# All scores in 64x64 tiles, key tails of four heads in one round, loads and engine order rearranged: cosine attention with a highway FFN behind it

## The chip, the cores and the metric

One core of one Trainium2 chip. The core has five engines that run their own instruction streams in order: PE (TensorE, matrix products; PEld is its weight load), DVE (VectorE), ACT (ScalarE), POOL (GpSimd) and SP (SyncE, here only a queue that starts transfers). A wait of an instruction holds up all that stands behind it on its engine. The metric is the device time of one execution in microseconds, the median over runs.

## The reference

Eight batches of twelve heads, 448 tokens, head dimension 64. Then a highway layer over the 3584 token rows of 768 numbers.

```python
q_n = q / (norm(q, axis=-1) + 1e-06);  k_n = k / (norm(k, axis=-1) + 1e-06)
scores = matmul(q_n, k_n^T) / tau                       # tau = 0.1
attn = softmax(scores);  a = matmul(attn, v)            # (8, 12, 448, 64)
x = a.transpose(0, 2, 1, 3).reshape(3584, 768)
H = maximum(x @ w_h, 0);  T = sigmoid(x @ w_t + b_t)    # 768 x 768 weights
out = T * H + (1 - T) * x
```

## The kernel before, in words

**Layout.** A head's 448 tokens are laid out as token = 7 l + j, with l = 0..63 on partitions and j = 0..6 (`NJ`) along the row. Two heads that differ in their last bit (s = 0, 1) share the 128 partitions. The twelve heads of a batch are three quads (g = 0..2); a quad holds the heads (t, s) with t, s = 0, 1. A pair p is the two heads t = 0, 1 at one s: six pairs a batch. Normalised and turned, a quad's queries and keys (`qT`, `kT`) have the two heads t on the two halves of the 128 partitions (64 numbers each) and tokens along the row.

**Stages of a batch.** Load q (started by SP), k and v (started by POOL, cast to half precision on the way; batch 0's k comes in full precision into `E` buffers by `ld_kf`). Squares on ACT (`norm`, `sq`), sums on DVE, the inverse root by Ln and Exp on ACT in batch 0 (`lnexp`) and by Newton steps on DVE else. `scale` multiplies q and k by it, mostly on POOL (`qn`, `kn`), for each quad in two halves t. `turn` transposes them: on PE with a copy by DVE, or by a transposing transfer in late batches (`QDMA`, `KDMA`). `scores` makes the products of keys and queries into PSUM banks (`B`, eight of them), ACT takes their exponentials into `E`; `attend` multiplies these with the values (`vp`, with a column of ones that yields the sum) on PE, and DVE divides. Batch 0 has its own versions (`attend0`) that cut the queries into four parts i. `ffn` then works on four row tiles a batch: it turns x, multiplies with `wt` and `wh` on PE, ACT takes a tanh, DVE and POOL combine, SP stores.

**Scores.** The 448 keys of a head are three chunks of 128 (c = 0..2) and a tail of 64. For each chunk of a pair, L496 issues two products of 64 rows by 128 columns, one for each head, on the two row halves of the array ("T" in the code). The tails of the pair go in one product over the whole array (L507): the keys' tail is held as a 128x128 block with zeros beside the two heads' parts, which is why `kn` has eight blocks of j, two half empty, that `zkn` fills with zeros, and why the scaling of k is two instructions (four and three blocks of j). Its exponentials are one tile `Et` a pair. In `attend`, each group c of query rows takes one product with `Et` over 130 columns (both heads at once, L521) and six with `E` over 65 columns (L526); the last 64 query rows go on column halves of the array ("C", L534). FFN products are whole-array (L682), its tail tiles on column halves (L679).

**Order.** All operations are recorded in a `Plan` with numbers, and `ORDER`, a table of these numbers made beforehand by a search, sets the order on every engine; `SLOTS` sets which buffer each tile takes. At emission some operations are also made to wait for one on another engine (`behind`): loads of q behind the latest ACT operation, a POOL operation behind the latest DVE operation, by two general rules.

**Counters of transfers.** In the built program each transfer that POOL starts raises one of eight counters, DMASW0 to DMASW7, in turn, and SP's and ACT's transfers use DMAHW0 to DMAHW7 in the same way. The ninth transfer takes the first counter again, and its instruction waits until the first transfer has landed.

**Start.** `WARM` = 18 products on zeros (`wz`) and `NF` = 39 further ones (L305) stand between the first real products of PE.

Of the kernel before, what the change touches and what calls it, by code (L numbers as in the profile page):

```python
# [20 lines left out]
66 1 67 342 68 0 69 3 72 71 7 70 5 42 61 339 23 19 75 74 64 21 44 52 20 51 22 55 79 9 83 43 2 6 14 13 81 82 73 80 8 85  # L21
86 16 84 15 63 39 341 87 76 88 12 95 96 60 108 25 33 56 31 11 38 24 107 46 89 40 114 113 17 37 109 32 4 90 53 30 111
10 97 18 112 98 93 115 118 110 353 54 116 174 91 137 124 117 94 357 92 29 142 173 175 28 122 105 123 99 340 177 59 119
180 354 121 100 125 120 133 127 128 349 141 126 48 138 26 34 350 154 58 178 347 129 140 153 176 131 578 139 144 143
358 78 134 132 130 106 150 149 45 179 348 155 101 102 343 152 151 156 47 77 186 355 57 359 135 189 181 190 182 192 191
351 360 136 361 50 362 183 146 62 104 103 363 364 145 41 147 36 365 148 184 185 187 27 352 383 198 188 158 162 356 377
378 579 161 165 166 157 35 167 164 159 193 194 163 202 49 382 201 345 168 381 379 169 197 195 196 203 204 209 170 160
206 200 199 212 380 210 171 222 172 346 221 205 384 207 266 234 226 208 267 344 211 224 225 233 223 227 366 367 213
809 214 235 286 271 272 385 368 287 369 370 584 215 371 372 581 592 216 236 228 268 291 217 386 269 238 218 404 585
219 387 245 270 237 273 588 593 248 220 246 229 403 393 240 239 292 430 230 288 247 416 388 242 231 398 293 65 389 432  # L30
241 392 391 394 583 397 289 589 232 243 279 280 413 274 417 431 290 244 427 306 275 281 429 395 428 307 249 415 410
414 316 317 412 250 396 252 390 586 318 594 401 424 253 587 276 580 582 590 402 450 254 376 277 425 311 255 595 312
278 256 808 260 426 259 411 319 451 294 262 591 375 433 261 1263 373 596 434 251 320 374 407 313 597 295 408 263 441
598 264 599 813 409 257 435 600 436 442 308 309 443 437 812 824 816 299 282 601 602 321 265 310 811 438 447 449 258
607 461 448 611 608 444 825 613 634 300 399 301 418 420 463 446 445 462 439 440 467 609 400 421 458 468 464 419 817
631 460 466 405 614 633 465 296 406 297 459 610 612 621 298 818 326 475 617 481 632 476 483 477 455 422 484 423 454
624 327 615 623 616 478 622 469 618 470 819 485 482 501 453 604 479 480 452 502 498 1036 456 302 500 495 619 472 471
487 499 496 492 486 663 488 603 820 620 606 497 605 494 457 473 489 283 637 640 474 490 491 493 814 815 641 505 625
504 503 642 822 638 639 506 643 507 328 508 528 645 329 646 821 509 626 333 334 644 657 647 304 284 303 664 674 330
628 823 335 651 627 648 650 697 680 649 658 566 547 654 826 659 676 681 675 652 660 532 314 827 810 828 829 1038 662  # L40
331 305 830 834 529 315 1037 1039 831 322 332 530 533 832 336 635 531 1035 655 636 843 698 661 513 656 534 1051 514
677 653 1270 671 323 510 511 540 665 337 541 667 678 515 679 629 512 672 673 837 1052 838 666 542 839 842 840 1043 691
685 859 630 855 1044 668 846 847 850 714 518 669 519 520 516 692 715 856 693 683 682 670 848 535 708 688 694 684 537
1271 538 695 1262 689 710 690 686 521 522 539 728 696 687 709 730 705 711 324 841 1045 712 523 567 707 702 713 568 729
833 536 543 1046 569 706 844 1047 701 731 700 338 551 699 732 703 835 851 725 1041 845 722 552 723 724 1048 553 718
559 560 716 717 544 887 726 870 1042 727 1049 889 704 736 719 735 734 890 852 857 733 720 561 721 325 849 285 858 737
556 557 836 860 738 864 872 871 891 888 777 867 861 558 1050 884 570 869 853 885 1274 572 573 886 854 545 865 866 881
898 571 883 1053 739 1054 517 873 758 874 1266 1055 1056 882 862 1057 1058 868 1490 1060 1059 548 863 549 924 900 899
550 892 894 877 876 1067 796 901 904 574 1275 895 878 740 893 1268 1065 1076 546 1087 1264 875 575 879 896 741 903 902
925 524 743 576 907 762 905 1272 526 1278 525 742 897 880 744 770 906 554 918 1279 915 555 908 771 763 916 759 527  # L50
1276 745 1040 1273 1064 760 1073 917 764 1070 1074 748 761 919 920 772 749 1066 1075 932 1082 1505 921 938 751 752 934
933 767 909 940 1083 750 910 941 911 1267 1269 1084 768 958 922 923 939 765 753 1277 935 959 562 769 1062 952 912 1280
766 936 929 797 1068 1063 1078 1489 798 913 914 953 937 746 955 949 577 1069 942 928 951 799 1061 781 782 1281 956 957
773 1265 954 950 563 1071 778 779 1072 926 774 927 1501 780 946 963 783 1111 1108 1282 943 945 1100 944 962 1493 564
# [809 lines left out]
```

## Time and profile before

| what | us |
|---|---|
| median of 3 runs | 254.03 (253.97 to 255.05) |
| span of the profiled execution, first to last instruction | 252.9 |
| the median over that span | 1.1 more |
| PE, DVE, ACT, POOL busy | 237.5, 208.0, 211.5, 184.0 |
| mean granted clock of PE | 0.990 |

The profile lists for each engine how long it was busy, the instructions in order of time, and who waited for whom. A busy PE includes products whose result is still under way, so short gaps do not show in its share. The profiled execution has no time of its own beside its span; the 1.1 us lie around it.

### The profile page before, as it was taken

How to read it: one execution, taken by the hardware profiler on the slowest of the kernel's cores; microseconds unless marked ns; L12 is line 12 of the kernel's file. 1: busy time of each engine (PE TensorE's matmuls, PEld its weight loads, DVE VectorE, ACT ScalarE, POOL GpSimd, SP SyncE). 2: the span in 40 equal slices, each digit the busy share in tenths (PEclk: the TensorE clock that was granted, in tenths of full speed). 3: DMA queues.
4: the chain of work that ended last, by engine and by line, in shares of the span. 5: the costliest groups of instructions: out<-in, count | busy, mean ns of one | idle time of the engine just before them, and what ended most of it. 6: DMA issues, size and time to landing. Idle time of an engine off the chain costs nothing.

```text
span 252.9 us, 7457 instructions
## 1 busy us (share of the span) xinstructions
PE 237.5 (94%) x2895; PEld 147.1 (58%) x2895; DVE 208.0 (82%) x462; ACT 211.5 (84%) x421; POOL 184.0 (73%) x261
## 2 busy tenths in 40 slices
PE   5959999999999999989999999999999999999990
PEld 2425776557756665645765566656656655675650
DVE  4977989999999999989899869689767665556983
ACT  3589999999999999989999999999997669981120
POOL 8369599959798979796989775878476983522540
PEclk9997999999999999999999999999999999999998
DMA  6999999999589999999999998999779588745755
GB/s 219 286 270 237 288 259 202 200 271 179 72 104 146 314 264 248 151 223 163 266 157 170 156 114 138 249 207 193 128 129 231 93 135 192 162 127 123 187 147 156
DMA packets 75892, 47.78 MB, mean 189 GB/s; under 512 B 51536, under 2 KB 72656, under 8 KB 75856
## 3 DMA queue, kind: packets, MB, share of 16 engines
q1 hardware_dynamic: 55568, 33.86, 59.2%
q0 software_dynamic: 19856, 12.68, 37.1%
q10 hardware_dynamic: 432, 0.75, 0.8%
q8 instruction: 22, 0.36, 0.6%
q14 instruction: 14, 0.11, 0.1%
HBM read 38.34 MB, written 11.01 MB: 195 GB/s over the span
## 4 chain that ended last, share of the span: by engine, by line
PE 68%; DMA 11%; ACT 8%; DVE 7%; issue 2%; POOL 2%; SPq 0%; DVEq 0%; POOLq 0%; ACTq 0%
PE B L682 26%; PE B L496 10%; PE B L526 8%; DMA xT<-x 7%; PE B L679 5%; PE B L521 3%; DMA E<-in_k_dram 3%; PE B L447 3%; ACT E L502 3%; PE B L534 3%; PE B L507 2%; PE B L573 2%; ACT sq L380 2%; PE B L305 2%; DVE hm L720 1%
## 5 line engine op out<-in xcount | busy, mean ns | idle before, releaser
L502 ACT ACTIVATE E<-B 128x448 f16<-128x448 f32 x252 | 122.8, 612 | 9.6 <-PE B L496 8.6
L682 PEld LDWEIGHTS <-xT 128*128 128x128 f16 x576 | 52.1, 98 | 39.6 <-issue 6.9
L752 POOL TENSOR_TENSOR os<-x,hm 128x384 f32<-128x384 f16 x53 | 47.6, 912 | 29.8 <-DVE hm L747 21.3
L682 PE MATMUL B<-wh,xT 128*128 128x384 f16 x288 | 56.7, 326 | 0.6 <-DMA xT<-x 0.6
L682 PE MATMUL B<-wt,xT 128*128 128x384 f16 x288 | 55.0, 326 | 1.8 <-DMA xT<-x 1.4
L432 POOL TENSOR_TENSOR kn<-kr,y 128x192 f16<-128x192 f16 (+1 forms) x84 | 45.8, 562 | 10.6 <-DVE y L409 6.1
L391 DVE TENSOR_REDUCE n<-sq 128x14 f32<-128x896 f32 (+1 forms) x50 | 51.2, 1039 | 2.8 <-ACT sq L380 2.6
L432 POOL TENSOR_TENSOR qn<-qr,y 128x448 f16<-128x448 f32 x47 | 43.9, 946 | 9.1 <-ACT y L420 4.4
L526 PE MATMUL B<-vp,E 128*128 128x65 f16 x756 | 38.7, 193 | 0.0
L724 ACT ACTIVATE tt<-z 128x768 f16<-128x768 f32 (+1 forms) x32 | 26.3, 821 | 14.6 <-DVE z L711 14.5
L720 DVE SCALAR_TENSOR_TENSOR hm<-B,x 128x384 f16<-128x384 f32 x53 | 28.8, 549 | 8.4 <-PE B L682 3.9
L526 PEld LDWEIGHTS <-E 128*128 128x128 f16 x756 | 33.7, 98 | 3.2
L496 PE MATMUL B<-qT,kT 64*128 64x448 f16 x252 | 34.8, 354 | 0.4 <-DVE hm L720 0.4
L711 DVE TENSOR_TENSOR z<-B,bias 128x384 f32<-128x384 f32 x48 | 25.8, 551 | 9.3 <-PE B L682 6.3
L521 PE MATMUL B<-vp,Et 128*128 128x130 f16 x126 | 28.1, 223 | 0.0
L380 ACT ACTIVATE sq<-qr 128x896 f32<-128x896 f32 (+1 forms) x24 | 24.1, 1022 | 3.5 <-DMA qr<-in_q_dram 3.5
L509 ACT ACTIVATE Et<-B 128x448 f16<-128x448 f32 x42 | 26.1, 631 | 0.4 <-PE B L507 0.4
L542 DVE SCALAR_TENSOR_TENSOR x<-B,rd 128x448 f16<-128x448 f32 x42 | 25.6, 618 | 0.9
L337 POOL DMA_DIRECT2D vr<-in_v_dram x32 | 21.9, 690 | 2.5 <-DVE z L711 2.5
L586 ACT ACTIVATE E<-B 128x512 f16<-128x512 f32 (+1 forms) x42 | 20.6, 607 | 0.9 <-POOL qn L432 0.5
L380 ACT ACTIVATE sq<-kr 128x896 f32<-128x896 f16 x17 | 17.0, 1041 | 1.1 <-DMA kr<-in_k_dram 1.1
L305 PE MATMUL B<-wz 128*128 128x512 f16 x39 | 14.7, 433 | 2.6 <-DVE wz L281 2.6
(81 smaller groups left out, 313.7 us busy)
## 6 DMA issues: line engine op xcount, KB each, us to landing
out_dram<-os SPq DMA_DIRECT2D x47, 192.0 KB, 3.3
qr<-in_q_dram SPq DMA_DIRECT2D x6, 1344.0 KB, 8.3
kr<-in_k_dram POOLq DMA_DIRECT2D x7, 672.0 KB, 11.6
vr<-in_v_dram POOLq DMA_DIRECT2D x16, 192.0 KB, 6.9
qr<-in_q_dram SPq DMA_DIRECT2D x6, 448.0 KB, 10.0
vr<-in_v_dram POOLq DMA_DIRECT2D x16, 144.0 KB, 7.7
out_dram<-os SPq DMA_DIRECT2D x15, 96.0 KB, 3.8
wt<-in_moe_w_t_dram POOLq DMA_DIRECT2D x1, 1152.0 KB, 24.4
```

The costliest lines, as they stand in the source:

```text
L380: nc.scalar.activation(dst, src, AF.Square, scale=sc)
L391: nc.vector.reduce_sum(R("n2", b)[:, c : c + 7 * n], a, axis=AX.X)
L432: ENG[eng].tensor_mul(N[:, :, t, :] if nm == "q" else N[:, lo > 0 : (lo > 0) + 2 * (hi - lo) - 1 : 2, t, :], source(nm, b, g)[:, t, 64 * l ...
L496: nc.tensor.matmul(R("B", ("S", n, c, t))[:, 0:S], lhsT=R("kT", i)[ln, s, 128 * c : 128 * c + 128], rhs=queries(ln), start=True, stop=True)
L502: nc.scalar.activation(R("E", n)[:, at : at + 7, :].rearrange("l j x -> l (j x)"), R("B", ("S", n, c, t))[:, 0:S], AF.Exp)
L509: op("ACT", f"expt {n}", lambda: nc.scalar.activation(R("Et", n).rearrange("l j x -> l (j x)"), R("B", ("St", n))[:, 0:S], AF.Exp), r=[("B ...
L521: nc.tensor.matmul(U[:, 2 * c : 2 * c + 2, :], lhsT=Et[:, 2 * c : 2 * c + 2, :].rearrange("l j x -> l (j x)"), rhs=vp[:, 6:8, 0:65], start ...
L526: nc.tensor.matmul(U[:, 2 * c + t, :], lhsT=E[:, at : at + 2, :].rearrange("l j x -> l (j x)"), rhs=vp[:, 3 * t + m, 0:65], start=False, s ...
L682: nc.tensor.matmul(P[:, 0:MH], lhsT=xT[:, cc, :], rhs=w_[:, cc, MH * mh : MH * mh + MH], start=(cc == 0), stop=(cc == CC - 1))
L720: op("DVE", f"hm {g} {mh}", lambda at=at, sl=sl, mh=mh: nc.vector.scalar_tensor_tensor(out=R("hm", g)[:, sl], in0=R("B", at)[:, 0:MH], sca ...
L724: op("ACT", f"th{nb} {g}", lambda: nc.scalar.activation(R("tt", g)[:, 0:W], R("z", g)[:, 0:W], AF.Tanh, scale=0.5), r=[("z", g), ("t0",)], ...
L752: op(eng, f"out {g} {mh}", lambda sl=sl, mh=mh: ENG[eng].tensor_add(R("os", g)[:, sl], xpart(mh), R("hm", g)[:, sl]), r=[("gg", g), xk], w ...
```

## The change

- Scores: one helper `score` issues four products of 64x64 for each chunk, one on each quarter of the array: head t on the row half t, key half h on the column half h. The 448-column products of a chunk are now four with 64 stationary columns in place of two with 128.
- Tails: the four heads of a quad have their tails done in one such round of four (`tails`, once a quad), into two banks; `Et` is one tile for each t, with the heads s on the partition halves. 42 whole-array products become 21 rounds of four. `vp` holds zeros in the other head's half.
- `attend`: each group c is eight products over 65 columns in place of one over 130 and six over 65.
- k stays in token order: seven blocks of j, no zeros, one scaling instruction for each half t, seven transposes in place of eight, copies of 896 columns in place of 1024, one transposing transfer a quad in place of two.
- Batch 0 scales half t = 0 of every quad on DVE (before: of quad 0 only).
- No further products on zeros (`NF` = 0); the 18 of `WARM` stand together at the start.
- Loads: ACT starts all three loads of batch 0's k, behind its table load (before: one ahead of it, two on SP). q comes in three loads a batch in all batches. v is loaded by s, not by t. POOL starts both weight loads, batch 2's k and two parts of batch 1's v ahead of its first own work, the identity `ident` for the transposes included.
- `ORDER` and `SLOTS` are new, and the two rules for `behind` give way to a table, `BEHIND`.

```diff
-66 1 67 342 68 0 69 3 72 71 7 70 5 42 61 339 23 19 75 74 64 21 44 52 20 51 22 55 79 9 83 43 2 6 14 13 81 82 73 80 8 85
+0 24 285 4 2 14 26 20 9 31 28 7 25 11 8 3 32 21 27 17 16 33 29 12 6 5 30 19 22 13 15 34 18 10 37 39 35 40 515 38 43 41
...
+BEHIND = dict(
...
+63:65 70:39 74:65 82:81 247:757 267:470 282:49 283:51 284:57 318:218 319:312 320:305 321:305 324:308 328:315 332:315
...
-    WARM, NF, NLATE = 18, 39, 2
+    WARM, NF, NLATE = 18, 0, 2
...
-    SCALE = {("q", 0, 0): ("DVE", "POOL"), ("k", 0, 0): ("DVE", "POOL")}
+    SCALE = {(nm, 0, g): ("DVE", "POOL") for nm in "qk" for g in range(NG)}
...
-        qr=(2, [128, 6, 448], FP32), kr=(3, [128, 6, 448], FP16), kn=(3, [128, 8, 2, D], FP16), vr=(2, [128, NH, 256], FP16),
+        qr=(2, [128, 6, 448], FP32), kr=(3, [128, 6, 448], FP16), kn=(3, [128, NJ, 2, D], FP16), vr=(2, [128, NH, 256], FP16),
...
-        Et=(3, [128, 7, 64], FP16), rd=(2, [128, 7], FP32), x=(3, [128, 7, MH], FP16),
+        Et=(4, [128, 7, 64], FP16), rd=(2, [128, 7], FP32), x=(3, [128, 7, MH], FP16),
...
-        for t, jj, j0, n in ((0, 0, 0, 4), (0, 1, 4, 3), (1, 0, 0, 3), (1, 1, 3, 4)):
+        for s, jj, j0, n in ((0, 0, 0, 4), (0, 1, 4, 3), (1, 0, 0, 3), (1, 1, 3, 4)):
...
-            for lo, hi in ((0, 7),) if nm == "q" else ((0, 4 - t), (4 - t, 7)):
...
-                op(eng, f"{nm}n{hi - lo} {b} {g} {t}", fn, r=[token(nm, b, g), ("y", b, nm, g)], w=[(nm + "n", i, t)])
+            op(eng, f"{nm}n7 {b} {g} {t}", fn, r=[token(nm, b, g), ("y", b, nm, g)], w=[(nm + "n", i, t)])
...
+    def score(out, o, w, K, Q, s, c):
+        for t, h in ((0, 0), (1, 1), (0, 1), (1, 0)):
+            ln = slice(64 * t, 64 * t + 64)
+            S_, j = (s, c + h * (4 - s)) if c < NC else (h, 3 + 3 * h)
+            nc.tensor.matmul(out[t][64 * h : 64 * h + 64, o[t] : o[t] + w], lhsT=K[ln, j, S_, :], rhs=Q[ln, :, S_, :], start=True, stop=True)
...
-                for t in range(2):
-                    ln = slice(64 * t, 64 * t + 64)
-                    nc.tensor.matmul(R("B", ("S", n, c, t))[:, 0:S], lhsT=R("kT", i)[ln, s, 128 * c : 128 * c + 128],
-                                     rhs=queries(ln), start=True, stop=True)
+                score([R("B", ("S", n, c, t)) for t in range(2)], (0, 0), S, R("kT", i), R("qT", i), s, c)
...
-            nc.tensor.matmul(R("B", ("St", n))[:, 0:S], lhsT=R("kT", i)[:, s, 384:512], rhs=queries(slice(0, 128)), start=True, stop=True)
+            score([R("B", ("St", i, t)) for t in range(2)], (0, 0), S, R("kT", i), R("qT", i), 0, NC)
...
-            nc.tensor.matmul(U[:, 2 * c : 2 * c + 2, :], lhsT=Et[:, 2 * c : 2 * c + 2, :].rearrange("l j x -> l (j x)"),
-                             rhs=vp[:, 6:8, 0:65], start=True, stop=False)
...
+                for m in range(NC + 1):
+                    lt = E[:, 7 * (2 * m + t) + 2 * c :][:, 0:2] if m < NC else R("Et", (i, t))[:, 2 * c : 2 * c + 2]
...
-                    ld_kf(g, "SP" if g else "ACT")
+                    ld_kf(g, "ACT")
...
-            ld_qk("q", b)
+            for g in range(NG):
+                ld_qk("q", b, [g])
...
-                elif o.held:
-
-                    behind(made[0], act)
...
+                last[o.seq] = made[-1]
+                if o.seq in BEHIND:
+                    behind(made[0], last[BEHIND[o.seq]])
```

**POOL at the start.** The names are those of the kernel: `kr_63` is the first buffer of k (batch 1's), `kr_64` the second (batch 2's), `vr_69` batch 0's v, `vr_70` batch 1's, `qn_83` and `kn_66` the scaled q and k of quad 0, `y_78` the inverse roots. Before:

```order
L322 DMA kr_63<-in_k_dram 128x6x448
L337 DMA vr_69<-in_v_dram 64x6x256 x2
L337 DMA vr_69<-in_v_dram 64x6x192 x2
L342 DMA wt<-in_moe_w_t_dram 128x6x768
L432 TENSOR_TENSOR qn_83<-qr_61,y_78 128x7x64 [waits DMAHW1_49,DVE_49,Activation_49]
L432 TENSOR_TENSOR kn_66<-E_94,y_78 128x4x64 [waits DMAHW0_49,DVE_49]
L432 TENSOR_TENSOR kn_66<-E_94,y_78 128x3x64
L432 TENSOR_TENSOR qn_84<-qr_61,y_78 128x7x64 [waits DMAHW2_49,DVE_49,Activation_49]
```

And now:

```order
L326 DMA kr_63<-in_k_dram 128x6x448
L341 DMA vr_69<-in_v_dram 64x6x192 x2
L341 DMA vr_69<-in_v_dram 64x6x256 x2
L346 DMA wt<-in_moe_w_t_dram 128x6x768
L346 DMA wh<-in_moe_w_h_dram 128x6x768
L326 DMA kr_64<-in_k_dram 128x6x448
L341 DMA vr_70<-in_v_dram 64x6x256 [waits DMASW0_49]
L341 DMA vr_70<-in_v_dram 64x6x192 [waits DMASW1_49]
masks.py:197 MEMSET ident 128x128
masks.py:199 ISA
masks.py:199 AFFINE_SELECT ident<-ident 128x128 [waits Pool_49]
L434 TENSOR_TENSOR qn_83<-qr_61,y_78 128x7x64 [waits DMAHW0_49,Activation_49]
```

Ten transfers stand ahead of POOL's first work in place of six; the ninth waits for the landing of the first (k of batch 1), the tenth for that of the second (the first part of batch 0's v), and the identity and the first scaling stand behind both.

**ACT at the start.** `sq` are squares, `B` a bank of scores whose exponentials go to `E`. Before:

```order
L380 ACTIVATE sq_73<-E_95 128x896 [waits DMAHW3_49]
L417 ACTIVATE tu_82<-n_76,eps 128x28 [waits DVE_49]
L420 ACTIVATE y_78<-tu_82 128x28 [waits Activation_49]
L380 ACTIVATE sq_74<-E_96 128x896 [waits DMAHW4_49]
L380 ACTIVATE sq_75<-kr_63 128x896 [waits DMASW0_49]
L380 ACTIVATE sq_73<-qr_61 128x896 [waits DMAHW5_49]
L380 ACTIVATE sq_74<-kr_63 128x896 [waits DVE_49]
L586 ACTIVATE E_94<-B_124 128x512 [waits PE_49]
```

And now:

```order
L384 ACTIVATE sq_73<-E_95 128x896 [waits DMAHW3_49]
L384 ACTIVATE sq_74<-qr_61 128x896 [waits DMAHW4_49]
L421 ACTIVATE tu_82<-n_76,eps 128x28 [waits DVE_49]
L424 ACTIVATE y_78<-tu_82 128x28 [waits Activation_49]
L384 ACTIVATE sq_75<-E_96 128x896 [waits DMAHW5_49]
L576 ACTIVATE E_94<-B_127 128x384 [waits PE_49]
L384 ACTIVATE sq_73<-kr_63 128x896 [waits DMASW0_49]
L576 ACTIVATE E_95<-B_123 128x512 [waits PE_49,Pool_49]
```

The first exponential has moved ahead of all squares of batch 1's k, which before filled ACT until PE's first scores were there.

**PE at a tail, in the middle of the program.** Before, a tail stands among whole-array products of the FFN:

```order
L682 LDWEIGHTS xT_108
L682 MATMUL B_124<-wt,xT_108 128x384
L507 LDWEIGHTS kT_90
L507 MATMUL B_122<-qT_89,kT_90 128x448 [waits DVE_49]
L682 LDWEIGHTS xT_105
L682 MATMUL B_128<-wh,xT_105 128x384 [waits DVE_49]
```

Now a round of four of one quad stands between products of another shape:

```order
L518 MATMUL B_125<-vp_72,Et_100 128x65
L460 LDWEIGHTS kT_91
L460 MATMUL B_129<-qT_89,kT_91 64x448 [waits Activation_49]
L460 LDWEIGHTS kT_91
L460 MATMUL B_124<-qT_89,kT_91 64x448 [waits Activation_49]
L460 LDWEIGHTS kT_91
L460 MATMUL B_129<-qT_89,kT_91 64x448
L460 LDWEIGHTS kT_91
L460 MATMUL B_124<-qT_89,kT_91 64x448
L667 LDWEIGHTS xT_107
L667 MATMUL B_123<-wh,xT_107 128x384 [waits DVE_49]
```

Tails have joined the products that need the array cut up. Over the whole order of PE, changes between the shapes (whole, row halves or quarters, column halves) go from 184 to 202.

More of the change, by code (lines that the diff above doesn't have):

```diff
@@ L801 @@
             for p in range(NP):
+                if p % 2 == 0:
+                    tails(b, p // 2)
                 scores(b, p)
@@ L812 @@
         with tc.manual_schedule():
-            before = act = None
+            last = {}
             for o in pl.ordered(ORDER, SLOTS):
@@ L817 @@
                 made = [i for i in nc.cur_bb.bb.instructions[made:] if i.engine == ENG[o.eng].engine]
-                if o.eng == "ACT":
-                    act = made[-1]
-                elif o.held:
-                    behind(made[0], act)
-                elif o.port and o.eng == "DVE":
-                    before = made[-1]
-                elif o.port and before is not None:
-                    behind(made[0], before)
-                    before = None
+                last[o.seq] = made[-1]
+                if o.seq in BEHIND:
+                    behind(made[0], last[BEHIND[o.seq]])
 _INS = ['q', 'k', 'v', 'tau', 'moe_w_h', 'moe_w_t', 'moe_b_t']
```

208 lines of the change are left out of this document (96 added, 112 removed), and 150 rows, old and new, of tables (BEHIND, ORDER).

## The prediction

> **What bounds the kernel now.** I read the busy shares first, then stretches of the span, then the start in order of time, since the change rearranges it, and last the steady rows of PE for prices.
>
> ```profile
> span 252.9 us, 7457 instructions
> PE 237.5 (94%) x2895; PEld 147.1 (58%) x2895; DVE 208.0 (82%) x462; ACT 211.5 (84%) x421; POOL 184.0 (73%) x261
> ```
>
> ```profile
> core 0: us, PE busy (x) PEld busy (x) DVE busy (x) ACT busy (x) POOL busy (x), PEclk, DMA share, GB/s
> 20.00:42.00 22.00, 22.00 (x330) 15.02 (x328) 19.87 (x51) 21.10 (x43) 18.64 (x28) 0.94 1.15 254
> 42.00:190.00 148.00, 145.15 (x1856) 90.45 (x1854) 132.28 (x286) 144.05 (x290) 122.31 (x174) 1.00 1.05 184
> 190.00:226.30 36.30, 35.86 (x453) 22.18 (x452) 22.97 (x51) 30.27 (x66) 22.61 (x29) 1.00 0.83 163
> ```
>
> From 20 us on two engines are full together: from 42 to 190 PE is busy 145.15 of 148 us and ACT 144.05. ACT then has 6.0 us of idle time up to 226.3, where its last exponential ends; behind that, the last batch's FFN and the stores take the rest of the span, 26.6 us. So a delay of ACT before 190 has little to vanish in, and saved PE work helps in full only behind 190. The start shows what the two are fed by.
>
> ```profile
> 14.77 0.95 ACT L380 ACTIVATE sq<-kr 128x896 f32<-128x896 f16 x1 [1.15 <-DMA kr<-in_k_dram]
> 15.62 0.93 ACT L380 ACTIVATE sq<-qr 128x896 f32<-128x896 f32 x1
> ...
> 17.30 0.57 ACT L586 ACTIVATE E<-B 128x512 f16<-128x512 f32 x1
> ...
> 21.53 3.98 ACT L586 ACTIVATE E<-B 128x512 f16<-128x512 f32 x8 [0.52 <-POOL qn L432]
> ...
> 1.46 1.01 POOL L322 DMA_DIRECT2D kr<-in_k_dram  x1
> 2.46 2.65 POOL L337 DMA_DIRECT2D vr<-in_v_dram  x4
> 5.07 0.88 POOL L342 DMA_DIRECT2D wt<-in_moe_w_t_dram  x1
> ...
> 9.22 0.94 POOL L432 TENSOR_TENSOR qn<-qr,y 128x448 f16<-128x448 f32 x1 [3.28 <-ACT y L420]
> ...
> 17.73 0.50 POOL L478 COPY vp<-vr 64x384 f16<-64x384 f16 x1 [1.95 <-DMA vr<-in_v_dram]
> ...
> 30.47 0.89 POOL L322 DMA_DIRECT2D kr<-in_k_dram  x1
> ...
> 11.45 0.55 PE L447 MATMUL B<-ident,qn 128*128 128x128 f16 x7
> ...
> 12.92 0.61 PE L447 MATMUL B<-ident,kn 128*128 128x128 f16 x8
> ...
> 14.32 0.23 PE L579 MATMUL B<-x 128*128 128x128 f16 x1 [0.57 <-DVE x L462]
> ...
> 19.32 1.03 PE L447 MATMUL B<-ident,kn 128*128 128x128 f16 x8 [2.54 <-POOL kn L432]
> ```
>
> POOL's first scaling ran at 9.22, when the roots `y` were there, and PE turned q at 11.45, k at 12.92, and made the first scores at 14.32. ACT waited for k of batch 1 until 14.77, POOL for the first part of v until 17.73: these are the landings of the first two transfers that POOL starts.
>
> ```profile
> DMA to landing us min/median/max: 13.3/13.3/14.7
> ...
> DMA to landing us min/median/max: 15.2/15.9/16.2
> ...
> wt<-in_moe_w_t_dram POOLq DMA_DIRECT2D x1, 1152.0 KB, 24.4
> ```
>
> The rows are k's first three loads, batch 0's v, and `wt`: 1.46 + 13.3 = 14.8, 2.46 + 15.2 = 17.7, and for `wt`, started right behind v at 5.1, 29.5.
>
> **POOL's start, the term that decides.** The changed order puts two parts of batch 1's v ahead of the identity and the first scaling. Their instructions take the first and second counter again, so POOL stands until k of batch 1 and then the first part of batch 0's v have landed. The identity no longer precedes k's start at 1.46; taken as 0.7 earlier, k lands at about 14.1. That first part of v is now one of the 144 KB parts, so I let it land between 16.3 and 17.7, and take 16.8. Starting a part of v costs 0.66 (2.65 for four): POOL is free at 17.5. The identity, which ran ahead of 1.46, is no longer hidden; I take 0.5 for it. Then come qn, 0.94, and kn. Where kn was two instructions of 256 and 192 columns, it is one of 448:
>
> ```profile
> L432 POOL TENSOR_TENSOR qn<-qr,y 128x448 f16<-128x448 f32 x47 | 43.9, 946 | 9.1 <-ACT y L420 4.4 <-DMA out_dram<-os 2.6 <-DVE vp L468 1.5
> L432 POOL TENSOR_TENSOR kn<-kr,y 128x256 f16<-128x256 f16 x42 | 25.4, 612 | 3.8 <-DVE hm L747 2.3 <-DVE y L409 1.2 <-DVE tt L726 0.3
> L432 POOL TENSOR_TENSOR kn<-kr,y 128x192 f16<-128x192 f16 x42 | 21.3, 512 | 6.7 <-DVE y L409 4.8 <-DVE tt L726 1.2 <-DVE hm L747 0.5
> L432 DVE TENSOR_TENSOR qn<-qr,y 128x448 f16<-128x448 f32 x1 | 1.0, 1046 | 0.0
> ```
>
> I price it at 0.95, nearest to qn. So q of quad 0 is scaled at 19.0 and k at 19.9. From the turn of k to the first scores went 1.4 us (12.92 to 14.32), and a product takes 0.2 to 0.3, so the first exponential stands at 21.6 in place of 17.30.
>
> ACT's lag is counted in work. From 14.77 to 21.53 (6.76 us) ACT idled 0.52. Of the rest the changed kernel has one square of q (0.93) already behind it, as it stands ahead of the first exponential. The other 5.3 us (three squares of k, one of q, three exponentials, a root) are still to do at 21.6. DVE stands too: its copy of the turned q is queued ahead of quad 1's scaling. It also takes four more scalings in batch 0, at most 4 x 1.05 = 4.2 us; in 20 to 42 it has 2.1 us idle, so part of this may show, and I put the hidden part's cost at 0 to 2 and take 0, since ACT has quad 0's fourteen exponentials (eight take 3.98) and four squares to run through meanwhile. **Term: +5.3**, between +2.9 (only the first landing is waited for: 2.4 less) and +7.
>
> POOL meets the same a second time: between the scalings of batch 1's quads stand loads that wait for `wt`, `wh` and k of batch 2. That k took from 30.5 to about 44 before, and is started behind the weights now, with a part of v less ahead of it: about 42. Quad 1 of batch 1 is then scaled by 48, and PE's order has its transposes ahead of batch 0's last quarter of scores. ACT has 36 exponentials of batch 0 and 7 of batch 1 ahead of those, at up to 0.5, and nine squares at up to 0.93, 28 to 30 us, and arrives there at about 50. The first delay thus covers the second: 0, at worst 3.
>
> **PE's work.** The steady rows:
>
> ```profile
> 200.40 0.22 PE L521 MATMUL B<-vp,Et 128*128 128x130 f16 x1
> 200.46 0.35 PE L526 MATMUL B<-vp,E 128*128 128x65 f16 x6
> 200.65 0.22 PE L521 MATMUL B<-vp,Et 128*128 128x130 f16 x1
> ...
> 201.49 0.28 PE L534 MATMUL B<-vp,E 128*64 128x65 f16 x6
> ...
> 201.76 0.65 PE L679 MATMUL B<-wh,xT 128*64 128x384 f16 x6
> 202.25 1.14 PE L679 MATMUL B<-wt,xT 128*64 128x384 f16 x12
> ...
> 206.45 0.35 PE L507 MATMUL B<-qT,kT 128*128 128x448 f16 x1
> 206.64 0.65 PE L682 MATMUL B<-wh,xT 128*128 128x384 f16 x3
> 207.22 0.74 PE L496 MATMUL B<-qT,kT 64*128 64x448 f16 x6
> 207.89 0.66 PE L682 MATMUL B<-wh,xT 128*128 128x384 f16 x3
> 208.39 0.35 PE L507 MATMUL B<-qT,kT 128*128 128x448 f16 x1
> ```
>
> From start to start, a tail takes 0.19 (206.45 to 206.64), and six row-half products 0.67 (207.22 to 207.89), that is three times 0.19 and 0.1 for the change of shape. No row shows four quarters. Bounds: row halves run two at a time at 0.19, and column halves too (six of 384 columns in 0.49, 201.76 to 202.25, 0.163 a pair, the whole-array pace of 207.89 to 208.39), though these read different rows of `wh` from the same partitions. Both kinds of sharing that a quarter needs are thus seen at full pace. A round of four lies between 0.19 and, if only two run at a time, 0.38; I take 0.19.
> - Chunks: 126 rounds at 0.19 before and after: 0.
> - Tails: 42 x 0.19 become 21 x 0.19: **-4.0**.
> - Changes of shape: 184 become 202, at 0.1: **+1.8**. The old tails stood among whole-array products and cost none.
> - `attend`: from 200.40 to 200.65 a group takes 0.25, of which the six of 65 columns 0.19 (200.46 to 200.65). Eight take 0.25: 126 x under 0.005 = **+0.4**.
> - k's transposes: 15 fewer, at most 0.08 each by the row at 11.45 (0.55 for seven): **-0.9**.
>
> Sum -2.7. Where ACT is as full as PE it can't show; where PE alone is full, behind 190, it can. I take half, **-1.3** (0 to -2.7).
>
> Costed at nothing: the 39 products on zeros (they stood where PE had nothing better; without them nothing covers the clock, below); fewer POOL scalings (42 x (0.61 + 0.51 - 0.95) = 7.1 us, but POOL is 73% busy); smaller copies on DVE; q in three loads, whose rows wait for buffers as one did; ACT's three starts of k behind the table load, late by that load's time, under a wait that ends 8 us later.
>
> **The clock.** Before, in the pause ahead of 19.32, it fell:
>
> ```profile
> 18.00:20.00 2.00, 0.68 (x7) 0.69 (x8) 1.20 (x2) 2.00 (x5) 2.00 (x5) 0.84 1.53 195
> 20.00:22.00 2.00, 2.00 (x14) 0.86 (x12) 1.54 (x2) 1.49 (x4) 2.00 (x3) 0.50 1.15 217
> ```
>
> It was 0.84 and 0.50, and the eight transposes at 19.32 took 1.03, against 0.61 for eight at 12.92. Now PE stands from about 8 to 19 and starts at half speed. The stretch loses the same again or up to 2 us, and ACT is the slower of the two there, so 0 to +2, I take 0. The Trainium skill, "TensorE: Matmul & The Clock Gate", Part 1, says that half rate is the default, and that a window of some 3.4 us of activity lifts it and an idle one brings it back. The trace agrees as far as these rows go: half speed up to 22 after a restart at 19.32. By that rule the estimate is 1.7 us lost at the restart, inside these bounds.
>
> **Sum.** 252.9 + 5.3 - 1.3 = 256.9 for the span; 1.1 lies around it in the median: 258.0.
>
> **Rivals.**
> 1. *The landing is early or isn't waited for.* Then the first exponential comes near 14 instead of 17.30, and PE's 2.54 us wait at 19.32 is gone: -2, and PE's -2.7: 249.5. For it: the load of q for batch 1 is held back longer, so k has less beside it. Against it: the part of v would have to land by 9. It decides below a landing of about 12.
> 2. *The delay is real but vanishes.* ACT idles 6.0 us between 190 and 226.3, where PE is full; if PE catches up by its saved 2.7 and by the time that zero products took, the lag shows only as 5.3 - 6 and PE's gain remains: 251.5 to 254. Against it: 97% of ACT in 42 to 190, in order.
> 3. *More goes wrong at the start*: the second wait at 3 and the clock at 2: 261 to 264.
> 4. *Quarters run two at a time*: 147 rounds x 0.19 = +28: 286. Against it: the column halves' row. The Trainium skill speaks against the change at this point: "TensorEngine Tiling (Array Packing)", Gotcha 2, says that column tiling excludes the fast weight load. The trace shows 16 column-half products with their loads in 0.27 us (201.49 to 201.76), 17 ns each, so four loads fit in 0.19 if loads of different tiles overlap as there.
>
> **How the numbers follow.** Forecast (254.8 to 261) 0.55; rival 1, 0.12; rival 2, 0.14, half of it faster and half within the bound; rival 3, 0.15; rival 4, 0.04. The bound, about what a measurement of this kernel tells from no change, is 0.5%, 1.27 us. Faster: 0.12 + 0.07 = 0.19. Same: 0.07 and 0.02 from the forecast's lower edge, 0.09. Slower: 0.72. The range leaves out rival 4, most of rival 1 and the ends of rival 3: 251 to 263. The forecast's own is 254.8 to 261.
>
> **What would show it.** Right: POOL idle from about 8 to 17 with DMA kr and vr as what ended it; PE's first transposes near 19; the first exponential near 21.6; a round of four at 0.19; ACT's last exponential at 229 to 231. Wrong: `ident` made before 10, or a round over 0.25, or ACT's idle time between 190 and its last exponential down from 6 to near 1 with the end unmoved.

## The result and the profile after

The changed kernel takes 281.13 us (median, 278.71 to 284.88), the kernel before 254.54 beside it: ratio 1.103, 95% interval 1.094 to 1.112. Forecast were 258.0 us and a range up to 263: the sign was right, 23 us were missing. (Single executions of most kernels here, the one before included, fall 1.5 to 5% behind by themselves; the medians count them, the ratios leave them out.)

Busy shares of the page after, and the three stretches shown of before, the last one drawn out to shortly before ACT's last exponential now ends (250.1), with the rest behind it. Columns: stretch and length; busy time and number of instructions of PE, weight load, DVE, ACT, POOL; granted clock, DMA share, GB/s.

```profile
span 276.9 us, 8586 instructions
PE 240.0 (87%) x3447; PEld 148.3 (54%) x3447; DVE 219.7 (79%) x459; ACT 212.7 (77%) x421; POOL 174.3 (63%) x210
```

```profile
20.00:42.00 22.00, 18.01 (x401) 13.99 (x390) 20.75 (x49) 19.68 (x41) 9.84 (x13) 0.67 1.15 260
42.00:190.00 148.00, 135.89 (x2000) 82.61 (x2000) 130.21 (x257) 132.46 (x261) 110.51 (x128) 0.97 0.96 167
190.00:248.00 58.00, 54.94 (x808) 34.01 (x809) 39.10 (x86) 46.32 (x101) 32.54 (x40) 0.97 0.79 134
248.00:276.90 28.90, 22.04 (x214) 13.61 (x210) 19.90 (x47) 7.01 (x12) 9.46 (x11) 0.94 0.59 148
```

From 42 to 190 PE and ACT were full before (145 and 144 of 148 us). Now they are busy 136 and 132, and POOL 111 in place of 122: every engine waits. DVE's total has risen from 208.0 to 219.7 us with three instructions fewer, so some of its instructions have become longer. The start, in order of time (start, duration, engine, line, instruction, and in brackets the idle time before it and what ended that):

```profile
14.18 1.44 POOL L341 DMA_DIRECT2D vr<-in_v_dram  x2 [6.81 <-DMA kr<-in_k_dram]
15.61 0.23 POOL masks.py:197 MEMSET ident<- 128x128 f16 x1
...
16.17 0.94 POOL L434 TENSOR_TENSOR qn<-qr,y 128x448 f16<-128x448 f32 x1
...
17.17 0.93 PE L450 MATMUL B<-ident,qn 128*128 128x128 f16 x7 [8.91 <-POOL qn L434]
...
20.29 0.49 ACT L576 ACTIVATE E<-B 128x384 f16<-128x384 f32 x1 [6.28 <-PE B L460]
```

POOL's stall is there as forecast: 6.81 us for k's landing. The second load followed at once. Where the rest went is seen first in one line of DVE, before and after (count; shortest, median and longest in ns; first and last start in us; shapes):

```profile
L747 DVE TENSOR_TENSOR hm<-tt,hm x30: 342/548/1290, 54.0 to 243.6; 128x768 f16<-128x768 f16 x23, 128x384 f16<-128x384 f16 x7
```

```profile
L732 DVE TENSOR_TENSOR hm<-tt,hm x30: 344/549/4347, 60.3 to 267.3; 128x768 f16<-128x768 f16 x23, 128x384 f16<-128x384 f16 x7
```

The longest one stands in the chain of waits (start, duration, what), and here it is with DVE, PE and POOL in order of time:

```profile
73.33 1.06 DVE kT L453 x2
74.39 4.27 DVE hm L732
78.66 0.53 DVE kT L453
...
79.34 0.64 DVE x L534
79.98 0.04 issue
80.02 0.96 PE B L460 x7
```

```profile
73.25 1.14 DVE L453 COPY kT<-B 128x896 f16<-128x896 f16 x2
74.32 4.35 DVE L732 TENSOR_TENSOR hm<-tt,hm 128x768 f16<-128x768 f16 x1
78.59 0.61 DVE L453 COPY kT<-B 128x896 f16<-128x896 f16 x1
...
79.25 0.53 PE L460 MATMUL B<-qT,kT 64*64 64x448 f16 x1 [2.17 <-DVE kT L453]
```

```profile
73.31 1.70 POOL L387 TENSOR_TENSOR sq<-kr 128x896 f32<-128x896 f16 x1
74.95 0.94 POOL L434 TENSOR_TENSOR qn<-qr,y 128x448 f16<-128x448 f32 x1
75.85 1.77 POOL L737 TENSOR_TENSOR os<-x,hm 128x384 f32<-128x384 f16 x2
77.58 0.70 POOL L341 DMA_DIRECT2D vr<-in_v_dram  x1
78.29 1.16 POOL L434 TENSOR_TENSOR qn<-qr,y 128x448 f16<-128x448 f32 x1
```

The gate `hm<-tt,hm` (L732, the last step of the FFN on DVE) takes 0.55 us as a rule. Here it was under way for 4.35, from the middle of POOL's square until 0.38 us after POOL was through with starting a load, while POOL ran without a gap. The copy of the turned k stood behind it on DVE, and PE's scores behind that copy: PE stood for 2.17 us. The two engines get in each other's way: the Trainium skill, "SBUF — State Buffer", section "SBUF: two separate sides", says that they share one pair of ports as an exclusive lock, held for the whole instruction, and that the loser blocks fully; a DVE instruction with two inputs in SBUF, as this gate has, meets it against a POOL instruction that reads SBUF. The trace agrees and shows more: the loser was not served when the square ended, but lost the next turns too, to a scaling and two sums. (It ended 1.04 us after the second sum, about twice its usual length; whether the start of the load held it up as well, the trace does not tell.)

The general rule of the kernel before (a POOL operation waits for DVE's latest one) had kept the two apart. Theory P: its replacement by the table `BEHIND`, which names 119 pairs, costs some 20 us. Its rivals: S, all of it follows from the late start; O, the new order itself costs it.

### The profile page after: what moved, and what is told of

It reads as the page before. It is cut to its first block, busy times and chain, and to the rows that moved or that the text cites. A ratio compares the mean times of both kernels' runs of the same rounds, so it can differ in the third digit from the quotient of the medians.

```text
span 276.9 us, 8586 instructions
## 1 busy us (share of the span) xinstructions
PE 240.0 (87%) x3447; PEld 148.3 (54%) x3447; DVE 219.7 (79%) x459; ACT 212.7 (77%) x421; POOL 174.3 (63%) x210
## 3 DMA queue, kind: packets, MB, share of 16 engines
q0 software_dynamic: 19856, 12.68, 34.2%
## 4 chain that ended last, share of the span: by engine, by line
PE 56%; DVE 13%; DMA 11%; ACT 9%; issue 4%; SPq 3%; POOL 2%; DVEq 0%; ACTq 0%; POOLq 0%
PE B L667 26%; PE B L460 11%; PE B L518 8%; ACT E L490 6%; DMA kr<-in_k_dram 5%; PE B L664 4%; DMA xT<-x 4%; DMA kT<-kn 3%; DVE n L395 3%; PE B L450 2%; PE B L590 2%; DVE hm L732 2%; PE B L526 2%; SPq L747 2%; ACT sq L384 1%
## 5 line engine op out<-in xcount | busy, mean ns | idle before, releaser
L460 PE MATMUL B<-qT,kT 64*64 64x448 f16 (+2 forms) x812 | 51.9, 333 | 10.6 <-DVE x L534 3.0
L667 PE MATMUL B<-wt,xT 128*128 128x384 f16 x288 | 56.8, 333 | 3.8 <-DMA xT<-x 3.1
L434 POOL TENSOR_TENSOR qn<-qr,y 128x448 f16<-128x448 f32 x45 | 42.5, 954 | 9.8 <-DVE hm L732 2.6
L434 POOL TENSOR_TENSOR kn<-kr,y 128x448 f16<-128x448 f16 x42 | 39.2, 944 | 14.5 <-DVE y L413 4.4
L460 PEld LDWEIGHTS <-kT 64*64 64x64 f16 x812 | 19.2, 111 | 29.7 <-issue 21.4
L518 PE MATMUL B<-vp,Et 128*128 128x65 f16 x252 | 34.8, 191 | 0.0
L501 ACT ACTIVATE Et<-B 128x448 f16<-128x448 f32 x42 | 22.7, 577 | 4.0 <-PE B L460 3.9
L576 ACT ACTIVATE E<-B 128x384 f16<-128x384 f32 (+2 forms) x42 | 20.2, 619 | 6.5 <-PE B L460 6.5
L518 PEld LDWEIGHTS <-Et 128*128 128x128 f16 x252 | 24.9, 99 | 0.0
```

Source lines behind the costliest of these rows:

```text
L434: ENG[eng].tensor_mul(R(nm + "n", i)[:, :, t, :], source(nm, b, g)[:, t].rearrange("l (j d) -> l j d", d=D), R("y", b)[:, c : c + NJ].unsq ...
L460: nc.tensor.matmul(out[t][64 * h : 64 * h + 64, o[t] : o[t] + w], lhsT=K[ln, j, S_, :], rhs=Q[ln, :, S_, :], start=True, stop=True)
L518: nc.tensor.matmul(U[:, 2 * c + t, :], lhsT=lt.rearrange("l j x -> l (j x)"), rhs=vp[:, 3 * t + m if m < NC else 6 + t, 0:65], start=(m == ...
L667: nc.tensor.matmul(P[:, 0:MH], lhsT=xT[:, cc, :], rhs=w_[:, cc, MH * mh : MH * mh + MH], start=(cc == 0), stop=(cc == CC - 1))
```

## The experiments

The tables' entries are given by name: `ldv` v loads (batch, part), `ldk` k loads, `ldwt` and `ldwh` the weights, `qn7`/`kn7` scalings (batch, quad, half).

**1. Loads moved far back.** Of POOL's order:

```diff
 ldwt, ldwh, ldk 2 0,
-ldv4 1 1 1, ldv3 1 1 0,
 ident, qn7 0 0 1, kn7 0 0 1, ldv4 1 0 0, kn7 0 1 1, qn7 0 1 1, ldv3 1 0 1, kn7 0 2 1,
+ldv4 1 1 1, ldv3 1 1 0,
```

> The changed kernel with one part undone: the two early loads of batch 1's v on POOL stand behind batch 0's scalings again, so that `ident` and the first scaling wait for no transfer. Theory S (all of the loss starts with the stall of 5 us at the start: the order was written for other times, and once POOL and ACT are 5 us late its waits no longer fall where they should): first exponential back near 17.3 us and the whole near 252 to 257 us. Theory P (the greater part of the loss is DVE standing still while POOL's squares and scalings run back to back, since the general wait of POOL's operations for DVE's latest one is gone): only the stall goes, 281.1 - 5 = 274 to 277 us, and gates (`hm<-tt,hm`, `tt<-tt`) of over 1.5 us remain in the trace. Theory O (the new order of the engines itself costs the rest): 274 to 277 us as well, without the long gates.

Measured: 283.6 us, ratio 1.112 (1.096 to 1.129). No gain, though the first exponential stood at 14.4: every theory had forecast less. POOL in order of time shows why:

```profile
31.84 0.95 POOL L441 TENSOR_TENSOR kn<-kr,y 128x448 f16<-128x448 f16 x1
38.15 0.70 POOL L348 DMA_DIRECT2D vr<-in_v_dram  x1 [5.36 <-DMA wh<-in_moe_w_h_dram]
42.79 0.66 POOL L348 DMA_DIRECT2D vr<-in_v_dram  x1 [3.94 <-DMA kr<-in_k_dram]
43.45 0.95 POOL L441 TENSOR_TENSOR qn<-qr,y 128x448 f16<-128x448 f32 x1
```

POOL's transfers take their eight counters in turn. The two loads that wait here, of batch 2's v, are its fifteenth and sixteenth, so they share counters with the seventh (`wh`) and the eighth (k of batch 2). They do so in the changed kernel too: there `wh` had landed at 34.2 when POOL came to the fifteenth load at 37.19, and k at 41.8, 0.3 us before the sixteenth started:

```profile
42.06 0.66 POOL L341 DMA_DIRECT2D vr<-in_v_dram  x1 [4.18 <-DVE y L413]
42.73 0.95 POOL L434 TENSOR_TENSOR qn<-qr,y 128x448 f16<-128x448 f32 x1
```

The roots `y` that the scaling behind it needs were ready at 42.0, so there the landing cost 0.7 us at most. In run 1 POOL comes earlier, meets both landings (37.9 and 42.5), and scales quad 1 of batch 1 at 43.45 in place of 42.73. A second wait had stood behind the first all along.

**2. The general rule in the place of the table** (with the rule for the q loads beside it), in the loop that emits the operations:

```diff
-                last[o.seq] = made[-1]
-                if o.seq in BEHIND:
-                    behind(made[0], last[BEHIND[o.seq]])
+                if o.eng == "ACT":
+                    act = made[-1]
+                elif o.held:
+                    behind(made[0], act)
+                elif o.port and o.eng == "DVE":
+                    before = made[-1]
+                elif o.port and before is not None:
+                    behind(made[0], before)
+                    before = None
```

> The changed kernel with the general rule of the kernel before in the place of the table `BEHIND`: each of POOL's shared-port operations waits for DVE's latest one of the order, and q loads wait for ACT's latest operation. Theory P: the long gates go, longest `hm<-tt,hm` of 768 columns back near 1.3 us, and the whole falls by 12 to 18 us, to 263 to 269 us, the stall of 5 us at the start remaining. Theory S: no gain, 278 to 284 us, since the late start is untouched. Theory O: 276 to 285 us; the rule's own waits in an order that was not made for them may even cost.

Measured: 264.0 us, ratio 1.025 (0.996 to 1.054), theory P; the ratio alone, on 254.5, makes it 261, which is 2 us below its range. The longest gate falls further than it said, to 0.74 us, and DVE's total with it:

```profile
PE 232.3 (87%) x3447; PEld 146.1 (55%) x3447; DVE 207.0 (78%) x459; ACT 212.1 (80%) x421; POOL 173.0 (65%) x210
```

```profile
L732 DVE TENSOR_TENSOR hm<-tt,hm x30: 345/548/744, 61.6 to 255.8; 128x768 f16<-128x768 f16 x23, 128x384 f16<-128x384 f16 x7
```

**3. Both edits.**

> Both edits: early loads moved back and the general rule in the place of `BEHIND`. Theory P with the stall: 257 to 264 us. Theory S: as with the loads alone, 252 to 257 us. Theory O: 270 us or more, which neither start nor port explains.

Measured: 264.1 us, ratio 1.028 (1.004 to 1.052). DVE is busy for 207.9 us and its longest gate takes 0.74, as in run 2. With the rule the moved loads gain nothing either: P holds, S falls for the whole, and POOL's first wait is not worth 5 us by itself. (With the rule as without it, POOL then stands 3.10 us for `wh` and 5.99 for k of batch 2.)

**4. The kernel before without its rule.**

```diff
-                elif o.port and before is not None:
-                    behind(made[0], before)
-                    before = None
```

> The kernel before without its general rule for POOL's and DVE's shared-port operations (the q loads' waits are kept). Theory P: the same collisions come in the old order: longest `hm<-tt,hm` or `tt<-tt` over 2 us, and 262 to 272 us against 254.5. Theory S and theory O: within 2 us of the kernel before, 253 to 257 us.

Measured: 277.8 us, ratio 1.091 (1.057 to 1.124), more than theory P's upper end. The other direction, in the old order with the old products:

```profile
PE 245.1 (89%) x2895; PEld 148.8 (54%) x2895; DVE 226.8 (83%) x462; ACT 213.0 (78%) x421; POOL 187.3 (68%) x261
```

```profile
L747 DVE TENSOR_TENSOR hm<-tt,hm x30: 342/552/3612, 53.4 to 265.6; 128x768 f16<-128x768 f16 x23, 128x384 f16<-128x384 f16 x7
```

Neither the start nor the order nor the shapes of the change are in this kernel, and the q loads' waits are kept: it is the rule for POOL and DVE that is worth this. DVE's work is longer by 18.8 us.

**5. Loads behind the first scalings, the order of the transfers kept.**

```diff
 ldwt, ldwh, ldk 2 0,
-ldv4 1 1 1, ldv3 1 1 0,
 ident, qn7 0 0 1, kn7 0 0 1,
+ldv4 1 1 1, ldv3 1 1 0,
 ldv4 1 0 0, kn7 0 1 1, qn7 0 1 1, ldv3 1 0 1, kn7 0 2 1
```

> The changed kernel with `ident` right behind POOL's last unblocked load and the two early loads of batch 1's v behind POOL's first two scalings; the order of POOL's transfers among themselves is that of the changed kernel, so that no other load takes the place of the one that waits (which moving them far back had done: a v load of batch 2 then waited until `wh` had landed at 36 to 38 us). Theory S1 (the 5 us of the start reach the end): first exponential at 14 to 15 us and the whole 4 to 6 us under the changed kernel, 273 to 277 us. Theory S2 (what is won at the start is lost again in later waits, above all for the shared port): 278 to 284 us.

Measured: 282.0 us, ratio 1.105 (1.095 to 1.115): S2. The first exponential stands at 14.59 in place of 20.29, and none of it reaches the end. The order of the transfers is unchanged, and yet POOL meets the same two waits as in run 1, so a changed order of the transfers is not what made them:

```profile
37.92 0.69 POOL L348 DMA_DIRECT2D vr<-in_v_dram  x1 [4.53 <-DMA wh<-in_moe_w_h_dram]
43.03 0.66 POOL L348 DMA_DIRECT2D vr<-in_v_dram  x1 [4.41 <-DMA kr<-in_k_dram]
```

(The wait for batch 1's k is not gone in these runs either: POOL stands at it for 2.54 us in runs 1 and 5, but behind its first two scalings.)

**6. The same with the general rule.**

> The same, and the general rule of the kernel before in the place of `BEHIND`. Theory S1: 4 to 6 us under the run with the rule alone (264.0), 257 to 260 us. Theory S2: 262 to 266 us. If port and start were all that the change lost, 250 to 255 us, the level of the kernel before or under it; what stays above 255 is the price of the order and of the parts costed at nothing.

Measured: 262.8 us, ratio 1.031 (1.028 to 1.034). Beside run 5 on the same chip this is the cleanest price of the rule, 19 us. S2 again for the start. POOL has met the same waits, for `wh` and for k of batch 2. The view names DVE for the second, but k landed at 43.2, which is 0.3 us before the load started, as in the changed kernel and runs 1 and 5; the `x` of L604 that it names neither reads nor writes a buffer of v:

```profile
35.40 0.69 POOL L348 DMA_DIRECT2D vr<-in_v_dram  x1 [1.78 <-DMA wh<-in_moe_w_h_dram]
43.48 0.66 POOL L348 DMA_DIRECT2D vr<-in_v_dram  x1 [7.39 <-DVE x L604]
44.15 0.95 POOL L441 TENSOR_TENSOR qn<-qr,y 128x448 f16<-128x448 f32 x1
```

**7. Quarters alone**, in the kernel before:

```diff
-                for t in range(2):
+                for t, h in ((0, 0), (1, 1), (0, 1), (1, 0)):
                     ln = slice(64 * t, 64 * t + 64)
-                    nc.tensor.matmul(R("B", ("S", n, c, t))[:, 0:S], lhsT=R("kT", i)[ln, s, 128 * c : 128 * c + 128],
+                    nc.tensor.matmul(R("B", ("S", n, c, t))[64 * h : 64 * h + 64, 0:S],
+                                     lhsT=R("kT", i)[ln, s, 128 * c + 64 * h : 128 * c + 64 * h + 64],
```

> The kernel before with each of its 252 full score products (64 rows, 128 columns of weights) split into two of 64 columns, four to a round; nothing else is changed. Theory Q1 (a round of four runs at the pace of the round of two): within 1.5 us of the kernel before, 253 to 256 us. Theory Q2 (two at a time): 126 rounds x 0.19 us and more of added PE time, 270 us or more.

Measured: 258.4 us (253.2 to 263.2), ratio 0.998 (0.993 to 1.002): no difference, Q1. Three rounds of four and the change of shape take 0.69 us (209.74 to 210.43) where three rounds of two took 0.67:

```profile
209.74 0.76 PE L496 MATMUL B<-qT,kT 64*64 64x448 f16 x12
210.43 0.66 PE L683 MATMUL B<-wh,xT 128*128 128x384 f16 x3
```

**8. The kernel before without the zero products** (`wf` issues nothing).

> The kernel before without its 39 zero products of the first 30 us; nothing else is changed. Theory C1 (they only fill time in which PE would wait): 253 to 255.5 us, granted clock in the first 30 us as in the kernel before or so. Theory C2 (they hold the clock up, and without them the first products run at half of it as in the changed kernel, 0.50 to 0.53 between 10 and 30 us): 256 to 261 us.

Measured: 254.4, 260.1, 261.3 and 263.4 us; the kernel before, in the same series, 253.7 to 261.4. Inconclusive for the whole: one execution shows no loss, two lie within the span of the kernel before, one above it. The trace (of the one with 261.3) has the clock at 0.53 from 10 to 20 us, where the kernel before has 0.97, so the zero products do hold it up; but DVE takes its first product of the FFN no later, at 43.8 against 44.4.

**9. Run 6, and batch 2's v later on POOL** (behind the eleventh scaling of batch 1).

```diff
 kn7 1 0 0, qn7 1 0 0,
-ldv4 2 0 0,
 kn7 1 0 1,
-ldv4 2 1 1, ldv3 2 0 1,
 qn7 1 1 1, ..., qn7 1 2 1,
+ldv4 2 0 0, ldv4 2 1 1, ldv3 2 0 1,
```

> The run with the loads behind and the general rule (262.8 us), and besides the first three loads of batch 2's v moved on POOL from among batch 1's first scalings to behind its tenth, so that nothing of batch 1's scaling stands behind a load that waits 1.8 us for `wh` and 7.4 us for DVE to free the buffer. Theory O (what is left above the kernel before is the order, and above all this queue): the stall of PE and ACT at 40 to 55 us goes and the whole falls by 3 to 5 us, to 257.5 to 260 us. Rival: ACT and PE wait there for other work, and it stays at 261.5 to 264 us.

Measured: 258.0 us, ratio 1.019 (1.012 to 1.025), theory O for this part. (The 7.4 us of the forecast were a wait for k's landing, as said.) POOL scales quad 1 of batch 1 at 39.72, right behind its roots (39.6), in place of 44.15. The times at which DVE first takes a product of the FFN tell where (run 6, then this run; shortest, median and longest in ns, then the first and the last start in us):

```profile
L712 DVE SCALAR_TENSOR_TENSOR hm<-B,x x53: 508/551/559, 54.7 to 250.3; 128x384 f16<-128x384 f32 x53
```

```profile
L712 DVE SCALAR_TENSOR_TENSOR hm<-B,x x53: 506/551/560, 50.3 to 245.0; 128x384 f16<-128x384 f32 x53
```

**10. Neither table nor rule.**

```diff
-                if o.seq in BEHIND:
-                    behind(made[0], last[BEHIND[o.seq]])
```

> The changed kernel with the table `BEHIND` left out and no rule in its place: POOL's operations and the q loads wait for data and buffers alone. Theory P (the table's pairs keep off some of the collisions, too few): as slow as the changed kernel or slower, 281 to 292 us, with more long gates. Theory W (the table's own waits, such as the 7.6 us that a residual sum on POOL waits for a Newton step of DVE, cost more than they save): 270 to 278 us.

Measured: 294.7 us, ratio 1.162 (1.154 to 1.170): P, somewhat above its range, and W falls.

```profile
PE 243.4 (83%) x3447; PEld 150.0 (51%) x3447; DVE 233.6 (79%) x459; ACT 213.5 (73%) x421; POOL 175.4 (60%) x210
```

```profile
L732 DVE TENSOR_TENSOR hm<-tt,hm x30: 345/552/5409, 63.4 to 284.8; 128x768 f16<-128x768 f16 x23, 128x384 f16<-128x384 f16 x7
```

So the table keeps off about half of what the rule keeps off. One order, three degrees of protection (rule, table, nothing): DVE busy 207.0, 219.7, 233.6 us; ratio 1.025, 1.103, 1.162. (Run 10 also frees the q loads, and its first FFN product is 3.4 us later than the changed kernel's.)

**11. Run 9, and batch 1's q earlier** (`ldq 1` behind the square of batch 0's second quad).

> The same as the run with batch 2's v later, and batch 1's three q loads moved forward on SP, behind the square of batch 0's second group, so that ACT no longer waits for them (2.5 us between 20 and 32 us). Theory O: 1 to 2.5 us less than that run, 255.5 to 258.5 us. Rival: the earlier q loads take bandwidth from `wt`, `wh` and k, or ACT then waits for POOL's halves; no change within 1 us, or slower by 1 to 2 us.

Measured: 259.6 us, ratio 1.023 (1.017 to 1.029). No gain: the rival.

**12. Run 9, and `ldwh`, `ldk 2 0` behind `ldv3 1 0 1` on POOL.**

> The run with batch 2's v later (258.0 us), and besides the loads of `wh` and of batch 2's k moved on POOL behind batch 1's v, as `wh` stood in the kernel before. Theory O2 (the first loads' order costs: `wh` takes bandwidth from batch 1's q, for which ACT's squares wait until 20.4 and 25 us): 1 to 3 us less, 255 to 257 us. Theory N (the loads are hidden there): 257.5 to 259 us. If `wh` now comes too late for the first FFN product (needed at 39 us), 259 to 262 us.

Measured: 260.7 us, ratio 1.019 (1.001 to 1.037). No gain within a wide interval; theory O2 isn't borne out. `wh` landed at 42.6, later than the 39 us named, but DVE took its first product of the FFN at 49.5, not behind run 9.

**13. Run 9, and 30 zero products**, in `turn`:

```diff
         def fn():
+            for _ in range({("q", 0): 10, ("k", 1): 6, ("q", 1): 6, ("k", 2): 4, ("q", 2): 4}.get((nm, i), 0)):
+                nc.tensor.matmul(R("B", at)[:, :], lhsT=wz[:, 0:128], rhs=wz[:, 128:640], start=True, stop=True)
             for j in range(NJ):
```

> The run with batch 2's v later (258.0 us), and 30 zero products of 512 columns ahead of the first transposes (10, 6, 6, 4 and 4), where PE waits for scaled halves. Theory C2 (the granted clock, 0.50 to 0.55 between 10 and 30 us and 0.76 up to 40, makes PE late from 27 to 38 us, where it sets the chain): clock over 0.85 from 20 us on, and 2 to 4 us less, 254 to 256 us. Theory C1 (the start waits for data, not for PE, as the run of the kernel before without its zero products was no slower in its best execution): 257 to 259.5 us.

Measured: 260.3 us, ratio 1.025 (1.015 to 1.035): no gain. Stretches of run 9, then of this run:

```profile
20.00:30.00 10.00, 6.83 (x118) 5.54 (x119) 7.75 (x21) 7.73 (x14) 4.55 (x6) 0.50 1.14 246
30.00:40.00 10.00, 9.65 (x228) 7.56 (x226) 8.22 (x24) 9.49 (x22) 3.06 (x5) 0.76 1.15 278
```

```profile
20.00:30.00 10.00, 6.97 (x114) 4.32 (x111) 7.29 (x17) 6.86 (x13) 3.70 (x5) 0.83 1.14 246
30.00:40.00 10.00, 8.87 (x238) 7.03 (x230) 8.83 (x28) 9.59 (x21) 3.62 (x4) 1.00 1.15 278
```

The clock rose from 0.50 to 0.83 and from 0.76 to 1.00, and ACT did no more in the stretch: C1, though 0.8 us above its range. (The zero products take time on PE themselves, which this run does not separate.)

**14. Runs 12 and 13 together.**

> Both edits of the start: `wh` and batch 2's k later, and the 30 zero products. Theories O2 and C2 together: 252 to 255 us, at the level of the kernel before or under it. O2 alone: 255 to 257 us. C2 alone: 254 to 256 us. Neither: 257 to 260 us.

Measured: 260.1 us, ratio 1.026 (1.021 to 1.031): neither of the two.

No version beats the kernel before; the best of the changed order is run 9.

## Why the prediction was wrong

- **The step that failed: `BEHIND` was costed at nothing.** It stood in the description of the change, but in no term of the sum, in no rival, and not among the parts with a named cover. It measured 19 us (run 6 against run 5), and 23 in the old order, within a wide interval (run 4). DVE's longer instructions are 12.2 us of the 19 (221.6 against 209.4 busy); the rest is waiting behind them, which was not split up. The profile of before could not show the price, since the rule held it off. But the prediction's own rows showed the scalings of k waiting for `hm` and `tt` (2.3, 0.3, 1.2 and 0.5 us), tiles that a scaling neither reads nor writes: those were the rule's waits, and they should have been asked what they buy.
- **POOL's start: right in the trace, wrong in the sum.** POOL was free at 15.6 (forecast 17.5; only the first landing was waited for, the lower end), first exponential at 20.29 (21.6). But the term of +5.3 was laid on the first wait, and taking that out of the way gained nothing (runs 1 and 5, with the rule runs 3 and 6), since POOL stands behind it for k of batch 2.
- **The second wait of POOL, put at 0 because the first delay covers it:** the landing was forecast well (about 42, and 41.8 in the trace), and the cover was real: the roots were ready at 42.0. What was missed is the reverse: the second wait covers the first as well, so that taking away the first alone gains nothing. With both out of the way (run 9) DVE's first product of the FFN comes at 50.3, in place of 54.7 (run 6) and 54.0 (run 2): 3.7 to 4.4 us for the two together.
- **What is left without `BEHIND` comes near the forecast in part by luck.** Run 2 is the change with the old rule: ratio 1.025, so 261 us against 258.0. But its loss is not the term's: its first product of the FFN is 9.6 us later than before's (54.0 against 44.4), and only some 4 of these are POOL's two waits. That run 9 stands at 258.0 is chance too.
- **Quarters at 0.19: right.** In the changed kernel twelve products and the change of shape take 0.70 us (201.37 to 202.07):

```profile
201.37 0.76 PE L460 MATMUL B<-qT,kT 64*64 64x448 f16 x12
202.07 0.27 PE L518 MATMUL B<-vp,E 128*128 128x65 f16 x3
```

 Run 7 confirms it over the whole kernel, against rival 4 and what Gotcha 2 of "TensorEngine Tiling (Array Packing)" in the Trainium skill let one fear.
- **PE's saving of -1.3 (0 to -2.7): in keeping with the runs, not shown by itself.** From DVE's first FFN product to the end, before takes 252.9 - 44.4 = 208.5 us, run 6 206.3 and run 9 205.4; the changed kernel takes 224.3. These 2 to 3 us hold all that the change does behind the start, and no run took tails, `attend` or transposes alone. (Fifteen transposes at the 0.08 named would be 1.2, not 0.9; after halving, that is 0.15 in the sum.)
- **The clock at 0: borne out as far as tested.** It was at 0.50 to 0.77 from 10 to 40 us, lifting it gained nothing (run 13), and where it fell to 0.53 in the old order the FFN began no later (run 8).
- **Rivals.** None held; rival 3 had the direction, but not the cause. Of the signs named, the end of ACT went furthest off: 250.1, not 229 to 231.

**Still open:** run 9 stands 1.9% above the kernel before. Its first FFN product comes 5.9 us later than before's (50.3 against 44.4), and 3 us are won behind it. Half of the delay is there before POOL's scaling: the roots of batch 1's quads 1 and 2 are ready at 39.6, before at 36.7. Batch 1's q, the place of `wh` and the low clock were each tried and brought nothing (runs 11 to 14); what in the new order of the start is the cause was not found.

## What to carry to other kernels

A wait that a kernel imposes on itself is a price already paid for something: when a change replaces it, first find what it keeps apart, and price its absence by the longest instructions of the engines concerned. Read DVE's durations, not only its idle time: an instruction held by a port counts as busy, and DVE's total rose with unchanged work. And a stall at the start of an in-order queue is worth only as much as the next stall behind it lets through: list all of them, with the time at which each ends, before one is priced.

## What the runs showed of the hardware

- A DVE instruction that meets POOL's unbroken work loses several turns: 4.35 us in the changed kernel, 5.41 without any wait, against 0.55; POOL's longest instruction there takes 1.70. The one of 5.41 stood from 95.08 to 100.49 through five scalings in a row and ended 0.42 us behind the last, where POOL first paused. The loss is the same from run to run of nearly the same order (4347, 4337 and 4342 ns in the changed kernel and runs 1 and 5).
- Such an instruction counts as busy: DVE's total went from 207.0 to 219.7 and 233.6 us with the same work, and its idle time does not show the loss.
- Eight counters make a load of POOL wait for the transfer eight places ahead of it, and with it all that stands behind on POOL: the sixteenth started at 42.06, 42.79, 43.03 and 43.48 (the changed kernel, runs 1, 5 and 6), each time 0.3 us after the eighth, k of batch 2, had landed (41.8, 42.5, 42.7 and 43.2). Moving two earlier loads did not change which transfers share a counter, only when POOL came to them.
